# Fused attention and MLP on one core: batch 0 goes through attention by token tiles with all heads

## The chip, the core and the metric

The kernel runs on one core of a Trainium2 chip. The metric is the device time of one execution in microseconds (us). The core has a matmul engine (TensorE, PE in the profile; PEld is its weight loading), two elementwise engines (VectorE, DVE; ScalarE, ACT), a programmable engine (GpSimd, POOL) and a queue engine that mostly issues transfers (SyncE, SP). Each engine runs its own instructions in program order, and semaphores tie them together. On-chip memory is SBUF (128 partitions); TensorE writes into PSUM, whose tiles come from small pools.

## The reference, cut to what matters

The input has 8 batches, 8 heads, 576 tokens and a head size of 64. Attention is causal with a bias from a running sum over tokens; its output, heads side by side, is normalized per token and goes through a two-layer MLP (512 to 2048 to 512) with a residual.

```
scores = scale * np.matmul(q, k.transpose(0, 1, 3, 2))
cum = np.cumsum(np.maximum(s, 0.0), axis=-1)
bias = -(cum[:, :, :, None] - cum[:, :, None, :])
scores = np.where(causal, -1000000000.0, scores + np.minimum(bias, 0.0))
scores = scores - np.max(scores, axis=-1, keepdims=True)
attn = np.exp(scores)
attn = attn / (np.sum(attn, axis=-1, keepdims=True) + 1e-09)
x = np.matmul(attn, v)            # then heads side by side: (8, 576, 512)
mu, var = mean and mean square deviation over the 512 of a token
xn = (x - mu) / np.sqrt(var + 1e-06) * g_ln
out = x + np.maximum(xn @ w_ch1, 0.0) @ w_ch2
```

## The kernel before

The program is written out in order by hand (`manual_schedule`), so each engine's queue is the order of the source. A token sequence of 576 is four tiles of 128 (`NF`) and one of 64 (`TL`).

*Scores.* For each head, `scores` (L304) multiplies keys by queries, transposed: 68 rows, 64 of the head and 4 for the bias. The running sum c is split into three bf16 parts (`c_hi`, `c_mid`, `c_lo`, L634 to L637); three rows beside k hold the parts against ones beside q, and one row of -1 stands against `c_hi`. The buffer `kq` holds these rows for four heads and alternates between two copies. Masked diagonal blocks get a second matmul with `ident` and `maskT` (`pe_mask`, for the first ten heads). ScalarE turns each bank of 512 columns into exponentials in `er` (L323). `pv` (L378) multiplies them with v, extended by a column of ones that gives the row sum; VectorE divides (L397, L399, L406).

*Filling kq.* Heads up to 19 come as pairs: rows are loaded, transposed on TensorE (`tr_kind`, L247) and evacuated by ScalarE and VectorE (`evac_pair`, L262). Bias rows are written by small transfers on SP (`aug`, L207; `constant_rows`, L215). Head 0's bias rows come from matmuls with a selection matrix `pick` (L646 to L660). Later heads have their bias in token rows (`rows`, with `cT` from `bias_tr` and `bias_rows`) and go through a transposing transfer on SP (`tr_rows`, L182), two to six heads ahead.

*The first eight heads.* The loop at L745 takes batch 0 head by head: scores of all 576 queries, a pair's transposes, fillers (`keep_warm`, L565, matmuls whose results nobody reads), then the PV of an earlier head. After the last head the statistics of its columns end, `ln_first` (L464) makes the mean and the normalized rows of all four tiles, and at n = 8 (L771) each tile is transposed (`ln_tr`, L478) and the first quarter of the MLP's first layer follows it, 128 columns at a time (`columns`, L778). The other parts of batch 0's MLP are units of four matmuls of 512 columns in `queue`, two for each head until head 16, and spread evenly over the heads after that (L809). A batch has 32 units: 16 of the first layer (`mlp1`, L493) and 16 quarters of the second (`mlp2`, L511).

*Buffers.* PSUM pools: `ps_s` 3 (scores), `ps_m` 2 (MLP and the first pairs' transposes), `ps_t` 2 (transposes, fillers), `ps_o` 1 (PV, or the bias transposes).

*Transfers.* SP carries float loads and the small bias rows; POOL's queue carries loads that cast to bf16 (`ld_cast`, `ld_cast_v`, `ld_w1`, `ld_w2`), in the order of the source[...].

The softmax here doesn't subtract the row's maximum and nothing guards it: scores larger than these inputs give would overflow.

## Time and profile before

| | us |
|---|---|
| Median of 3 runs | 366.84 |
| The runs | 366.84, 366.32, 371.82 |
| Profiled execution, whole | 368.54 |
| Profiled execution, span from first to last instruction | 366.8 |
| TensorE busy | 355.0 |
| VectorE busy | 202.9 |
| ScalarE busy | 191.3 |
| GpSimd busy | 164.9 |

The span is what the views of the trace divide; the profiled execution's own time is 1.7 us longer. A busy TensorE counts the fillers too, and the ends of matmuls are modelled. In a row of the timeline the first number is the start in the span, the second the length; "L" is the line in the kernel; a bracket names the idle time before an instruction and what ended it. "128*128 128x512" is the stationary operand (rows * columns) and the moving one.

### The profile page before, as it was taken

What the parts mean: (1) busy time and instruction counts of PE and PEld (TensorE: products, weight loads), DVE (VectorE), ACT (ScalarE), POOL (GpSimd) and SP (SyncE); (2) the same over time, 40 slices, a digit from 0 to 9 for tenths busy, and PEclk for the clock granted to TensorE, in tenths of its full rate; (3) what the DMA queues carried; (4) which work ended last, traced back from release to release, by engine and by line L of the source; (5) the groups of instructions that cost most, each with busy time, mean ns of one, the idle gap of its engine ahead of it and who ended that gap; (6) DMA issues with size and microseconds to landing.
All of it is one profiled execution on the core that took longest, in us unless ns stands there. A gap on an engine that the chain in (4) does not pass through costs nothing.

```text
span 366.8 us, 8315 instructions
## 1 busy us (share of the span) xinstructions
PE 355.0 (97%) x3017; PEld 197.1 (54%) x3067; DVE 202.9 (55%) x535; ACT 191.3 (52%) x367; POOL 164.9 (45%) x447
## 2 busy tenths in 40 slices
PE   8998999999999999999999999999999999999995
PEld 3677555565555555555455555555555554444444
DVE  7697789684357554944384547743675483112211
ACT  5895988467732673367534753476337522501410
POOL 8854468667633656344675563554852101000000
PEclk9999999999999999999999999999999999999999
DMA  8999999999965999599979986798830011011013
GB/s 144 162 195 178 202 211 193 163 240 176 183 146 141 206 199 181 104 215 163 188 176 213 194 183 140 189 191 182 174 102 2 0 59 57 1 58 59 0 31 86
DMA packets 156653, 52.17 MB, mean 142 GB/s; under 512 B 143641, under 2 KB 151940, under 8 KB 156612
## 3 DMA queue, kind: packets, MB, share of 16 engines
q1 hardware_dynamic: 138868, 43.08, 55.5%
q0 software_dynamic: 17344, 8.03, 18.9%
q8 instruction: 24, 0.39, 0.5%
q10 hardware_dynamic: 400, 0.52, 0.4%
q14 instruction: 17, 0.14, 0.2%
HBM read 37.11 MB, written 9.44 MB: 127 GB/s over the span
## 4 chain that ended last, share of the span: by engine, by line
PE 72%; DVE 7%; DMA 6%; SPq 4%; POOL 4%; issue 3%; ACT 3%; POOLq 0%; ACTq 0%
PE py L515 26%; PE ph L497 25%; PE pot L389 6%; SPq L164 3%; PE sc L312 3%; PE sa L312 3%; PE sb L312 3%; DMA rowtmp<-in_q_dram 2%; PE idle L568 2%; DMA vtmp<-in_v_dram 2%; DVE xn L451 2%; PE trx L484 2%; DVE stats L423 1%; POOL er L331 1%; ACT er L323 1%
## 5 line engine op out<-in xcount | busy, mean ns | idle before, releaser
L515 PE MATMUL py<-w_bf,hT 128*128 128x512 bf16 (+1 forms) x565 | 132.1, 373 | 1.6 <-DVE yo L524 0.4
L497 PE MATMUL ph<-xT,w_bf 128*128 128x512 bf16 x478 | 116.4, 379 | 1.1 <-DVE yo L524 0.2
L507 ACT ACTIVATE hT<-ph 128x512 bf16<-128x512 f32 x102 | 61.0, 598 | 64.4 <-PE ph L497 64.4
L515 PEld LDWEIGHTS <-hT 128*128 128x128 bf16 x592 | 53.5, 98 | 49.1 <-issue 0.9
L497 PEld LDWEIGHTS <-w_bf 128*128 128x128 bf16 x560 | 50.1, 97 | 51.3 <-issue 2.9
L323 ACT ACTIVATE er<-sa 128x512 bf16<-128x512 f32 x64 | 38.2, 597 | 70.9 <-PE sa L312 50.1
L331 POOL TENSOR_SCALAR_AFFINE_SELECT er<-er 128x128 bf16<-128x128 bf16 x216 | 59.7, 300 | 22.5 <-ACT er L323 22.3
L505 DVE TENSOR_SCALAR hT<-ph 128x512 bf16<-128x512 f32 x38 | 26.3, 692 | 56.7 <-PE ph L497 49.0
L176 POOL CAST rows<-rowtmp 128x512 bf16<-128x512 f32 (+1 forms) x55 | 33.5, 609 | 50.7 <-DMA rowtmp<-in_q_dram 46.0
L312 PEld LDWEIGHTS <-kq 68*128 68x128 bf16 x452 | 33.4, 97 | 27.4 <-issue 1.7
L389 PEld LDWEIGHTS <-er 128*128 128x128 bf16 x960 | 37.5, 98 | 14.9 <-issue 0.7
L389 PE MATMUL pot<-v_bf,er 128*128 128x65 bf16 x960 | 40.2, 193 | 0.5 <-PE sd L355 0.3
L397 DVE RECIPROCAL rinv<-pot 128x5 f32<-128x5 f32 x64 | 12.3, 192 | 49.2 <-PE pot L389 48.9
L323 ACT ACTIVATE er<-sc 128x512 bf16<-128x512 f32 x64 | 39.2, 612 | 0.0
L323 ACT ACTIVATE er<-sb 128x512 bf16<-128x512 f32 x64 | 38.4, 599 | 0.3 <-PE sb L312 0.2
L524 DVE SCALAR_TENSOR_TENSOR yo<-py,rstd,xb 128x512 f32<-128x512 f32 x32 | 23.9, 748 | 26.2 <-PE py L515 19.7
L399 DVE TENSOR_TENSOR xb<-pot,rinv 128x256 f32<-128x256 f32 x64 | 27.2, 425 | 2.2
L102 POOL CAST v_bf<-vtmp 128x512 bf16<-128x512 f32 (+1 forms) x30 | 18.5, 617 | 19.6 <-DMA vtmp<-in_v_dram 19.5
L439 POOL TENSOR_TENSOR rstd<-rstd,mhalf 128x4 f32<-128x4 f32 (+1 forms) x8 | 8.8, 1095 | 38.0 <-DVE rstd L438 37.9
L312 PE MATMUL sc<-kq 68*128 68x256 bf16 (+1 forms) x216 | 25.3, 229 | 0.3
L423 DVE BATCH_NORM_STATS2 stats<-xb 128x6 f32<-128x128 f32 (+2 forms) x100 | 25.3, 313 | 0.4
L312 PE MATMUL sb<-kq 68*128 68x64 bf16 (+1 forms) x172 | 24.5, 244 | 0.9 <-DMA kq<-rows 0.6
(101 smaller groups left out, 322.1 us busy)
## 6 DMA issues: line engine op xcount, KB each, us to landing
out_dram<-yo SPq DMA_DIRECT2D x32, 256.0 KB
vtmp<-in_v_dram SPq DMA_DIRECT2D x24, 256.0 KB
rowtmp<-in_k_dram SPq DMA_DIRECT2D x44, 128.0 KB
rowtmp<-in_q_dram SPq DMA_DIRECT2D x44, 128.0 KB
w_bf<-in_moe_w_ch_dram POOLq DMA_DIRECT2D x8, 512.0 KB, 10.7
kp<-in_k_dram POOLq DMA_DIRECT2D x9, 144.0 KB, 6.8
qp<-in_q_dram POOLq DMA_DIRECT2D x9, 144.0 KB, 7.0
v_bf<-in_v_dram POOLq DMA_DIRECT2D x8, 128.0 KB, 8.1
```

The source lines that it names most:

```text
L176: nc.gpsimd.tensor_copy(out=r[0:pn, :, :, 0:D], in_=loaded.pop(("rows", gam, t))[0:pn])
L312: nc.tensor.matmul(a[:, c + a0 - q0 : c + a1 - q0], lhsT=k_cols(b, h, kb), rhs=cols, start=True, stop=not (pe_mask and diag),)
L323: nc.scalar.activation(out=e[:, o : o + 512], in_=a, func=ACT.Exp, scale=scale)
L331: nc.gpsimd.affine_select(out=e[:, o : o + P], in_=e[:, o : o + P], compare_op=ALU.is_ge, fill=0.0, base=0, pattern=[[1, P]], channel_mult ...
L389: nc.tensor.matmul(pot[:, t, :], lhsT=e[:, o : o + P], rhs=vv[:, kb, h, :], start=(kb == 0), stop=(kb == last),)
L399: nc.vector.tensor_tensor(out=xb[b][:, :, hs], in0=pot[:, 0:NF, 0:D], in1=rinv[:, 0:NF].unsqueeze(2).to_broadcast([P, NF, D]), op=ALU.mult,)
L423: nc.vector.bn_stats(out=st[b][:, t, part, :], in_=x[:, lo:hi])
L497: nc.tensor.matmul(ph, lhsT=w1_bf[:, kd, fb * P : (fb + 1) * P], rhs=xT[:, kd, :], start=(kd == 0), stop=(kd == KD - 1),)
L505: nc.vector.tensor_scalar_max(out=hT[:, fb, :], in0=ph, scalar1=0.0)
L507: nc.scalar.activation(out=hT[:, fb, :], in_=ph, func=ACT.Relu)
L515: nc.tensor.matmul(py[0], lhsT=hT[:, fb, t * P : (t + 1) * P], rhs=w2_bf[:, fb, c0:c1], start=(fb == 0), stop=(fb == FB - 1),)
L524: nc.vector.scalar_tensor_tensor(out=yo, in0=py[0], scalar=rs, in1=x[:, c0:c1], op0=ALU.mult, op1=ALU.add)
```

## The change

Batch 0 no longer goes head by head. Its token rows of k and q are laid beside each other for all heads in `rowb` (128 tokens, 5 tiles, 8 k heads and 8 q heads, 68 columns), with the bias in columns 64 to 67: constants by `memset`, the parts of c by transposes and two copies for each tile (`bias_tr`, `bias_cols`). For this c is summed and split in three column ranges (0 to 128, to 256, to 576). A tile's 16 row blocks of 68 columns are transposed on TensorE (`tr_tile`) and one copy for four heads, 1024 elements a partition, moves them into `kq` (`evac_tile`).

The order is then by query tile t: scores of all eight heads for this tile against keys 0 to t (`tile_bank`, four blocks to a bank), PV for four heads at once (`tile_pv`) with division and statistics, norm of this tile (`ln_xn`, `ln_tr`), and the pieces of the first MLP layer for this tile (`piece`: four column blocks of 128 hidden units). Two of the layer's four quarters are done as pieces, so batch 0 leaves 24 units in `queue` instead of 28, and head 8 runs two units in the common loop. The last 64 tokens have their own functions (`last_bank`, `last_keys`, `last_pv`).

The selection matmuls of head 0, the constant rows, `aug` for the first two groups, `ln_first` and the transfers of pairs 0 to 3 are gone. k and q of tile 0 come as floats on SP with a cast on ScalarE, the other tiles by casting loads on POOL's queue. `aug(2)`, pair 4's transposes and `bias_rows` stand at the end of the new part, pairs 8 and 9 are loaded one head earlier, and the loop starts at head 8. The diff, cut:

```diff
+    rowb = const.tile([P, NT, 2 * H, KA], BF16, name="rowb")
...
+    def tile_src(kind, t):
+        pn = P if t < NF else TL
+        src = k if kind == "k" else q
+        return src[0, :, t * P : t * P + pn, :].rearrange("h s d -> s h d")
+
+    def tile_dst(kind, t):
+        pn = P if t < NF else TL
+        u = "kq".index(kind)
+        return rowb[0:pn, t, u * H : (u + 1) * H, 0:D]
+
+    def ld_tile(kind, t):
+        tmp = stage.tile([P, H, D], F32, name="tiletmp", tag="st")
+        nc.sync.dma_start(out=tmp, in_=tile_src(kind, t))
+        loaded[kind, t] = tmp
+
+    def cast_tile(kind, t, eng):
+        copy_on(eng, tile_dst(kind, t), loaded.pop((kind, t)))
+
+    def ld_cast_tile(kind, t):
+        nc.gpsimd.dma_start(out=tile_dst(kind, t), in_=tile_src(kind, t))
...
+    trc = ps_o.tile([P, 3, NT, BH], BF16, name="trc", tag="pot")
+
+    def bias_tr(t):
+        pn = P if t < NF else TL
         for j, src in enumerate((c_hi, c_mid, c_lo)):
-            for t in range(NT):
-                pn = P if t < NF else TL
-                nc.tensor.transpose(
-                    tr[0:pn, j, t, :], src[:, t * P : t * P + pn], ident[0:BH, 0:BH]
-                )
-        return tr
+            nc.tensor.transpose(
+                trc[0:pn, j, t, :], src[:, t * P : t * P + pn], ident[0:BH, 0:BH]
+            )
+
+
+    def bias_cols(t0, t1, pn=P):
+        nc.vector.tensor_copy(
+            out=rowb[0:pn, t0:t1, 0:H, D + 1 : KA],
+            in_=trc[0:pn, :, t0:t1, 0:H].rearrange("p j t x -> p t x j"),
+        )
+        nc.vector.tensor_copy(out=rowb[0:pn, t0:t1, H : 2 * H, D], in_=trc[0:pn, 0, t0:t1, 0:H])
+
+
+    def cum_scan(c0, c1):
+        nc.vector.tensor_tensor_scan(
+            out=c_sc[:, c0:c1],
+            data0=c_one[:, c0:c1],
+            data1=c_in[:, c0:c1],
+            initial=0.0 if c0 == 0 else c_sc[:, c0 - 1 : c0],
+            op0=ALU.mult,
+            op1=ALU.add,
+        )
+
+    def cum_relu(c0, c1):
+        nc.vector.tensor_scalar(
+            out=c_in[:, c0:c1],
+            in0=c_in[:, c0:c1],
+            scalar1=0.0,
+            scalar2=1.0 / scale,
+            op0=ALU.max,
+            op1=ALU.mult,
+        )
+
+    def cum_split(c0, c1):
+        x, y, hi, mid, lo = (a[:, c0:c1] for a in (c_sc, c_in, c_hi, c_mid, c_lo))
+        nc.vector.tensor_copy(out=hi, in_=x)
+        nc.vector.tensor_tensor(out=y, in0=x, in1=hi, op=ALU.subtract)
+        nc.vector.tensor_copy(out=mid, in_=y)
+        nc.vector.tensor_tensor(out=lo, in0=y, in1=mid, op=ALU.subtract)
...
-        if g < 5:
-            tr = ps_m.tile([P, S], BF16, name="trqk", tag="m")
-        else:
-            tr = ps_t.tile([P, S], BF16, name="trqk", tag="tr")
+        tr = ps_t.tile([P, S], BF16, name="trqk", tag="tr")
...
+        pool, tag = (ps_m, "m") if b == 0 else (ps_t, "tr")
+        tr = pool.tile([P, KD, P], BF16, name="trx", tag=tag)
...
-    ld_pair("k", 0)
-    ld_pair("q", 0)
-
-    ONE2 = 1.0019378662109375
-    NEG2 = -1.0058441162109375
+    ld_tile("k", 0)
+    ld_tile("q", 0)
...
-    keep_warm(12)
+    keep_warm(9)
...
+    for t in range(1, NF):
+        ld_cast_tile("k", t)
+        ld_cast_tile("q", t)
+        ld_cast_v(0, t - 1)
+    ld_cast_v(0, NF - 1)
+    ld_w1(0)
+    ld_cast_tile("k", NF)
+    ld_cast_tile("q", NF)
+    ld_cast_v(0, NF)
+    ld_w1(1)
+    ld_cast_pair(4)
+    nc.gpsimd.memset(v_bf[1][:, 0:NF, :, D : D + 1], 1.0)
+    nc.gpsimd.memset(v_bf[1][0:TL, NF, :, D : D + 1], 1.0)
+    for i in range(2):
         nc.gpsimd.memset(v_bf[i][TL:P, NF, :, :], 0.0)
     nc.gpsimd.memset(er[TL:P, :, OD : OD + TL], 0.0)
     nc.gpsimd.memset(er[:, :, OD + TL : EW], 0.0)
+    ld_cast_pair(5)
+    ld_w1(2)
     for t in range(NT):
+        ld_cast_v(1, t)
+    ld_w1(3)
...
+    def tr_tile(t):
+        pn = P if t < NF else TL
+        for g in range(2):
+            tr = ps_m.tile([P, 2, G, P], BF16, name="trt", tag="m")
+            for u in range(2):
+                for hh in range(G):
+                    nc.tensor.transpose(
+                        tr[0:KA, u, hh, 0:pn],
+                        rowb[0:pn, t, u * H + g * G + hh, :],
+                        ident[0:pn, 0:pn],
+                    )
+            trt[t, g] = tr
...
+    def evac_tile(t, g, eng):
+        pn = P if t < NF else TL
+        copy_on(
+            eng,
+            kq[g][0:KA, :, :, t * P : t * P + pn],
+            trt.pop((t, g))[0:KA, :, :, 0:pn],
+        )
+    def tile_bank(t, g, i):
+        a = ps_s.tile([P, 512], F32, name="st", tag="s")
+        for c in range(4):
+            hh, kb = divmod(4 * i + c, t + 1)
+            nc.tensor.matmul(
+                a[:, c * P : (c + 1) * P],
+                lhsT=kq[g][0:KA, 0, hh, kb * P : (kb + 1) * P],
+                rhs=kq[g][0:KA, 1, hh, t * P : (t + 1) * P],
+                start=True,
+                stop=kb < t,
+            )
+            if kb == t:
+                nc.tensor.matmul(
+                    a[:, c * P : (c + 1) * P], lhsT=ident, rhs=maskT, start=False, stop=True
+                )
+        o = (0, 2, 6, 0)[t] + g * (t + 1) + i
+        nc.scalar.activation(out=er_slot(o), in_=a, func=ACT.Exp, scale=scale)
...
+    def tile_pv(t, g):
+        pot = ps_t.tile([P, G, D + 1], F32, name="pot0", tag="tr")
+        for hh in range(G):
+            for kb in range(t + 1):
+                i, c = divmod(hh * (t + 1) + kb, 4)
+                o = (0, 2, 6, 0)[t] + g * (t + 1) + i
+                nc.tensor.matmul(
+                    pot[:, hh, :],
+                    lhsT=er_slot(o)[:, c * P : (c + 1) * P],
+                    rhs=v_bf[0][:, kb, g * G + hh, :],
+                    start=(kb == 0),
+                    stop=(kb == t),
+                )
+        rinv = small.tile([P, NT], F32, name="rinv", tag="rinv")
+        nc.vector.reciprocal(out=rinv[:, 0:G], in_=pot[:, :, D])
+        x = xb[0][:, t, g * 256 : (g + 1) * 256]
+        nc.vector.tensor_tensor(
+            out=x.rearrange("p (h d) -> p h d", d=D),
+            in0=pot[:, :, 0:D],
+            in1=rinv[:, 0:G].unsqueeze(2).to_broadcast([P, G, D]),
+            op=ALU.mult,
+        )
+        nc.vector.bn_stats(out=st[0][:, t, g, :], in_=x)
...
+    def last_bank(g, i):
+        a = ps_s.tile([P, 512], F32, name="st", tag="s")
+        for hh in range(G):
+            for w in range(2):
+                kb, c = 2 * i + w, (2 * hh + w) * TL
+                nc.tensor.matmul(
+                    a[:, c : c + TL],
+                    lhsT=kq[g][0:KA, 0, hh, kb * P : (kb + 1) * P],
+                    rhs=kq[g][0:KA, 1, hh, NF * P : S],
+                    start=True,
+                    stop=True,
+                )
+        nc.scalar.activation(out=er_slot(8 + 2 * g + i), in_=a, func=ACT.Exp, scale=scale)
...
+    def last_pv(g):
+        pot = ps_t.tile([P, G, D + 1], F32, name="pot0", tag="tr")
+        for hh in range(G):
+            for kb in range(NT):
+                h = g * G + hh
+                if kb < NF:
+                    c = (2 * hh + kb % 2) * TL
+                    e = er_slot(8 + 2 * g + kb // 2)[:, c : c + TL]
+                    vv = v_bf[0][:, kb, h, :]
+                else:
+                    e = er_slot(0)[0:TL, h * TL : (h + 1) * TL]
+                    vv = v_bf[0][0:TL, kb, h, :]
+                nc.tensor.matmul(
+                    pot[0:TL, hh, :], lhsT=e, rhs=vv, start=(kb == 0), stop=(kb == NF)
+                )
+        rinv = small.tile([P, NT], F32, name="rinv", tag="rinv")
+        nc.vector.reciprocal(out=rinv[0:TL, 0:G], in_=pot[0:TL, :, D])
+        nc.vector.tensor_tensor(
+            out=xm[0][0:TL, g * 256 : (g + 1) * 256].rearrange("p (h d) -> p h d", d=D),
+            in0=pot[0:TL, :, 0:D],
+            in1=rinv[0:TL, 0:G].unsqueeze(2).to_broadcast([TL, G, D]),
+            op=ALU.mult,
+        )
...
+    def piece(c, t, eng):
+        ph = ps_m.tile([P, 4, P], F32, name="ph", tag="m")
+        cols = slice(t * P, (t + 1) * P)
+        for j in range(4):
+            fb = 4 * c + j
+            for kd in range(KD):
+                nc.tensor.matmul(
+                    ph[:, j, :],
+                    lhsT=w1_bf[:, kd, fb * P : (fb + 1) * P],
+                    rhs=xTs[0][:, kd, cols],
+                    start=(kd == 0),
+                    stop=(kd == KD - 1),
+                )
+        dst = hT[:, 4 * c : 4 * c + 4, cols]
+        if eng == "act":
+            nc.scalar.activation(out=dst, in_=ph, func=ACT.Relu)
+        else:
+            nc.vector.tensor_scalar_max(out=dst, in0=ph, scalar1=0.0)
...
+    R = (P, 2 * P, S)
+    cum_relu(0, R[0])
+    cum_scan(0, R[0])
+    cum_split(0, R[0])
+    cast_tile("k", 0, "act")
+    cast_tile("q", 0, "act")
+    cum_relu(R[0], S)
+    bias_tr(0)
+    bias_cols(0, 1)
+    cum_scan(R[0], R[1])
+    cum_split(R[0], R[1])
+    keep_warm(1)
+    tr_tile(0)
+    evac_tile(0, 0, "act")
+    bias_tr(1)
+    evac_tile(0, 1, "dve")
+    bias_cols(1, 2)
+    cum_scan(R[1], S)
     keep_warm(2)
+    banks(0, 0, 0)
+    banks(0, 1, 0)
+    tr_tile(1)
+    evac_tile(1, 0, "act")
+    evac_tile(1, 1, "dve")
+    cum_split(R[1], S)
+    tile_pv(0, 0)
+    tile_pv(0, 1)
+    banks(1, 0, 0, 1)
+    for t in (2, 3, 4):
+        bias_tr(t)
+    bias_cols(2, NF)
+    bias_cols(NF, NT, TL)
+    banks(1, 1, 0, 1)
+    tr_tile(2)
+    evac_tile(2, 0, "act")
+    evac_tile(2, 1, "dve")
+    keep_warm(2)
+    banks(2, 0, 0, 1, 2)
+    tile_pv(1, 0)
+    tile_pv(1, 1)
+    ln_xn(0, 0)
+    tr_tile(3)
+    evac_tile(3, 0, "dve")
+    evac_tile(3, 1, "dve")
+    banks(2, 1, 0, 1, 2)
+    ln_xn(0, 1)
+    keep_warm(2)
+    banks(3, 0, 0, 1)
+    tile_pv(2, 0)
+    ln_tr(0, 0, "act")
+    banks(3, 0, 2, 3)
+    tile_pv(2, 1)
+    ln_xn(0, 2)
+    piece(0, 0, "dve")
+    banks(3, 1, 0)
+    ln_tr(0, 1, "act")
+    banks(3, 1, 1)
+    piece(0, 1, "dve")
+    banks(3, 1, 2, 3)
+    tile_pv(3, 0)
+    ln_tr(0, 2, "act")
+    piece(0, 2, "dve")
+    tile_pv(3, 1)
+    ln_xn(0, 3)
+    tr_tile(4)
+    evac_tile(4, 0, "act")
+    evac_tile(4, 1, "dve")
+    piece(1, 0, "act")
+    last_bank(0, 0)
+    last_bank(0, 1)
+    piece(1, 1, "dve")
+    last_bank(1, 0)
+    ln_tr(0, 3, "act")
+    last_bank(1, 1)
+    piece(1, 2, "dve")
+    last_keys()
+    aug(2, nc.sync)
+    piece(0, 3, "act")
+    tr_pair(4)
+    evac_pair("k", 4, ("dve", "dve"))
+    evac_pair("q", 4, ("act", "act"))
+    piece(1, 3, "dve")
+    last_pv(0)
+    last_pv(1)
+    bias_rows(trc)
+    queue = batch_units(0)[8:]
```

## The prediction

> **What bounds the kernel now.** I read the page first, then the chain of waits up to 80 us, then busy time by windows cut at stages, then the timelines of TensorE and VectorE to 72 us.
>
> ```profile
> span 366.8 us, 8315 instructions
> ...
> PE 355.0 (97%) x3017; PEld 197.1 (54%) x3067; DVE 202.9 (55%) x535; ACT 191.3 (52%) x367; POOL 164.9 (45%) x447
> ```
>
> TensorE sets the end, but part of its 97% is filler (`keep_warm`, tile `idle`). Windows (columns: stretch, length, busy PE, PEld, DVE, ACT, POOL, clock, DMA share, GB/s) show that only the start can give anything:
>
> ```profile
> 11.04:28.44 17.40, 16.33 (x262) 12.24 (x264) 13.76 (x39) 16.34 (x34) 12.37 (x20) 1.00 1.79 179
> 28.44:31.65 3.21, 2.83 (x23) 1.52 (x24) 3.04 (x16) 2.24 (x3) 1.45 (x3) 1.00 2.15 154
> 63.46:80.58 17.12, 16.93 (x160) 9.75 (x160) 13.37 (x41) 8.86 (x20) 9.55 (x26) 1.00 0.93 192
> ```
>
> From 63 us TensorE is full with real work (16.93 of 17.12). From 11 to 28.4 ScalarE is full (16.34 of 17.40: the exponentials and half the evacuations). Then the chain leaves TensorE (start, length):
>
> ```profile
> 1.26 5.30 PE idle L568 x12
> ...
> 20.50 0.45 PE pot L389 x15
> ...
> 28.38 0.52 DVE stats L423 x4
> ...
> 30.84 1.43 DVE xn L451 x2
> 32.31 0.40 PE trx L484 x4
> ...
> 34.00 0.89 PE ph L782 x16
> ```
>
> The norm of batch 0 waits for its last head; TensorE meanwhile runs 15 transposes and fillers. The state to compare is the top of head 9:
>
> ```profile
> 29.76 1.67 PE L568 MATMUL idle<-zeros 128*128 128x512 bf16 x7 [0.16 <-issue]
> ...
> 39.24 0.42 PE L255 MATMUL trqk<-ident,kp 96*128 96x96 bf16 x6
> ```
>
> At 39.24 batch 0's attention and head 8's scores are done, and 27 of batch 0's 32 MLP units remain. The change reaches the same place with 22 (24 queued, two run in head 8). A unit is four 512-column matmuls, 8 in 1.73 us, so 0.864. Break-even is 39.24 + 5 x 0.864 = 43.56 us.
>
> [...] The change transposes rows 68 wide and uses 64-wide stationaries for the last tile; the trace has just three such loads, in the bias transposes (groups by form, 28 to 30 us: count, busy, mean ns):
>
> ```profile
> L227 PE MATMUL trc<-ident,c 64*128 64x64 bf16 x12 | 0.9, 192 | 0.3 <-DVE xm L406 0.3
> L227 PE MATMUL trc<-ident,c 64*64 64x64 bf16 x3 | 0.6, 213 | 0.0
> ```
>
> [...] these 15 run from 28.44 to 29.53, 1.09 us, where 15 matmuls of 65 columns with wide weights take 0.45 (the chain above, L389). So (1.09 - 0.44)/3, about 0.21 us more, for each narrow load standing among wide ones. [...] here the first 12 fillers take 5.30 us, half speed. [...] the trace's bf16 copy of 512 from PSUM took 0.42 us against 0.69 for a float one, so 1024 elements cost 0.70.
>
> **The change part by part.**
> *Start.* Bias, head 0's selection matmuls, constant rows and early `aug` DMAs go; scan and split come in column ranges. c lands at 3.94 as now; 128 columns need relu 0.22, scan 0.40, split 1.05 (scaled from 0.60, 1.35, 2.5 for 576), bias transposes at 5.7. k and q of tile 0 come as 256-byte pieces, 1024 each:
>
> ```profile
> q1 hardware_dynamic: 2849, 0.71, 108.4%
> ...
> q0 software_dynamic: 4129, 0.57, 213.8%
> ```
>
> The first line is 58 to 61 us: 950 such packets per us. With issue at 1.5 and 2.1 as now and the landing delay of the old pairs (k used at 5.61), q lands near 6.6; cast 0.6; first transposes 7.3, against 6.97 now. The second line is 9 to 13 us: about 1030 packets per us from POOL's queue, so a k, q or v tile costs 1.0 us. Ten of them from POOL, issued from 1.9 on at 0.9 each, land from 7.6 (k1) to 16.1 (v3); tile t's transposes want theirs at 10.4, 16.7, 19.9, so the transfers are covered by 2 to 6 us. w1 parts land by 19 and 23, first used at 25.7. `gb` comes earlier; nothing waits for it.
>
> *TensorE's work from 7.3 to the top of head 9*, at 0.056 us per 128 columns (L782, 16 in 0.89) and 0.031 per 64/65:
> 80 row transposes x 0.060 + 5 runs x 0.2 = 5.8; 80 score blocks and 32 masks x 0.056 = 6.2; last tile's scores 1.0, keys 1.1; 80 PV x 0.031 = 2.5; last PV 40 x 0.060 + 0.2 = 2.6; norm transposes 0.9; eight pieces x 16 x 0.056 = 7.1; bias 0.4; fillers 1.3; pair 4 0.5; head 8 with two units 2.75. Sum 32.2. [...]
>
> What this replaces up to 39.24: 25 fillers after the first 12 (0.216 each, 5.4), head 0's selection matmuls and gaps of some 3 us go, which is all there is to win; the pairs' transposes (eight sets at 0.26, 2.1) become 5.8, scores 5.8 become 8.3, PV 3.6 becomes 5.1.
>
> *Waits.* VectorE gets a long serial queue. What it will do for every tile it does now once for every head (timeline of VectorE: start, length):
>
> ```profile
> 23.12 0.20 DVE L397 RECIPROCAL rinv<-pot 128x5 f32<-128x5 f32 x1 [0.34 <-PE pot L389]
> 23.35 0.42 DVE L399 TENSOR_TENSOR xb<-pot,rinv 128x256 f32<-128x256 f32 x1
> ...
> 23.88 1.39 DVE L423 BATCH_NORM_STATS2 stats<-xb 128x6 f32<-128x256 f32 x4
> ...
> 35.15 0.42 DVE L100 COPY xT<-trx 128x512 bf16<-128x512 bf16 x1 [1.57 <-PE trx L484]
> 36.49 1.29 DVE L799 TENSOR_SCALAR hT<-ph 128x512 bf16<-128x512 f32 x2 [0.92 <-PE ph L782]
> ```
>
> Each product waits for its reciprocal and each statistic for its product, so a PV drain is 0.22 + 0.44 + 0.36 = 1.0, eight of them; a norm 0.18 + 0.74, four; five evacuations 0.70 (last 0.4); five piece drains 0.64; splits 1.75 for 320 columns. Followed in program order:
> tile 0/1 evacuations and ScalarE's (1024 elements, 0.98) 0.7; the 320-column split stands behind tile 1's evacuation at 12.4 and ends at 14.2, the bias transposes of tiles 2-4 wait 1.3; then two drains and the bias copies until 16.6, tile 2's row transposes wait 1.5; its evacuation 0.3; tile 3's evacuation stands behind two drains and a norm and ends at 23.6, its scores wait 1.2; pieces wait for a PSUM buffer of two behind norm and drains 0.8 + 0.8; tail 0.3, 0.2 and 0.7 (last PV, behind pair 4's evacuation). Sum 7.8. ScalarE has 20 us idle in this stretch; exponentials no longer bound it.
>
> *Sum.* 7.3 + 32.2 + 7.8 = 47.3, 3.8 past break-even. Only 9 fillers run before a gap: [...] I take 0.4. Total +4.2.
>
> *Edits at nothing.* `aug(2)` now waits for the last keys' scores (39.1): four SP issues of 0.6 and about 2 us of landing end at 43.5, head 8 needs them at 44.7; less cover costs what is late. Nothing useful stands behind them on SP. `bias_rows` (2.0 on VectorE) moves from head 9 to before head 8, beside scores and a unit. POOL's later loads keep order; `rstd`'s power holds POOL until 34, w2 is first used about 55. Heads 16-19 have 8 units instead of 13: row transposes for head 20, last issued at 71.56 and used at 80.58, lose 4.3 of 9.0 us cover.
>
> The profiled execution took 368.54 (span 366.8): it becomes 372.7. The median of the runs shown, 366.84, becomes 371.0.
>
> **Rivals.**
> *Narrow loads serialize (slower).* If each waits until the previous matmul has left, as both sides of the three did, a step is 0.144 (64 columns) or 0.17 (128). Row transposes 64 x 0.17 + 16 x 0.144 = 13.2 (+7.4), keys 2.3 (+1.2), last PV 5.8 (+3.2): +11.8, of which 1.4 fills waits: 381.4. It passes 2% (7.3 us; about what a measurement of this kernel can tell) from 0.09 per step. For: no narrow load in the trace overlaps. Against: both sides of each were switches, which a run has once. If instead a run costs nothing but its switch, 369.
> *Transfers late.* If POOL's tile loads take 1.6 times as long, sharing engines with k, q and `gb`, tiles 2 and 3 start late by 2.8: 373.8. Against: nothing else is queued after 7 us.
> *Faster.* If VectorE keeps up and the 7.8 of waits vanish, 39.5 against 43.56: 362.8; it decides where waits stay under 4.0. For: VectorE's work is less than TensorE's. Against: two PSUM buffers and the program's order.
>
> **How the numbers follow.** Forecast 371.0, chance 0.53, own range 368 to 374; serial 0.31; late transfers 0.08; faster 0.06; else 0.02. Range 366 to 382 leaves out the fast case and the serial tail. Slower by over 2% (374.2): 0.31, part of the transfers, the forecast's tail: 0.38; faster by over 2%: 0.03; the rest 0.59.
>
> **What would show it.** Row transposes starting at 7.3; 16 of them in 1.2 us (2.7 if serial); tile 2's start near 16.7 waiting on VectorE's bias copy, not on DMA; last PV 1.3 us a half; head 9 at 47. I am wrong if head 9 comes before 44 or after 52, or if heads 16-19 show idle TensorE.

## The result and the profile after

The changed kernel takes 378.59 us (median of 4 runs, 377.44 to 380.07) against 366.73 for the kernel before beside it (4 runs): a ratio of 1.033, 95% interval 1.0284 to 1.0375. The ratio leaves out one slow run of the kernel before, of 371.82. The change makes it 11.9 us slower; the forecast was +4.2 (371.0, range 366 to 382). Its profiled execution took 378.56. The page of the changed kernel: span and the granted clock in 40 slices of 9.4 us (a 9 is full speed, or nearly so):

```profile
span 376.9 us, 8560 instructions
...
PEclk9899969999999999999999999999999999999999
```

The clock has dips in the second and the sixth slice. The windows of the changed kernel (columns as in the prediction) put them in two short stretches:

```profile
16.03:24.01 7.98, 6.76 (x84) 5.72 (x85) 4.36 (x14) 4.16 (x7) 6.05 (x12) 0.79 1.50 188
...
42.84:53.07 10.23, 8.43 (x62) 4.85 (x62) 4.19 (x10) 1.95 (x4) 0.85 (x2) 0.69 1.19 183
```

The stretch of the last line holds the last PV, a hole and head 8. The top of head 9 comes at 53.07, where the forecast had 47.3 and the break-even point was 43.56. The chain of waits of the changed kernel (start, length) says what the hole is:

```profile
40.84 1.15 SPq L223
...
42.03 5.62 DMA kq<-c
...
47.78 0.58 PE sa L347
```

The path leaves every compute engine. It runs from the last keys' scores (39.26) to SP's four issues of `aug(2)` (from 39.38) and then lies 5.62 us in the last of the four transfers (four rows of 1152 bytes each), while the last PV is done 1.8 us before head 8 can start. TensorE's timeline for the same stretch, and one run of row transposes:

```profile
10.43 1.05 PE L658 MATMUL trt<-ident,rowb 128*68 128x128 bf16 x16
11.32 0.42 PE L704 MATMUL pot<-v_bf,er 128*128 128x65 bf16 x8
...
42.84 3.14 PE L765 MATMUL pot<-v_bf,er 128*64 128x65 bf16 x40 [0.85 <-ACT kq L96]
47.78 0.58 PE L347 MATMUL sa<-kq 68*128 68x512 bf16 x1 [1.80 <-DMA kq<-c]
...
49.44 1.91 PE L516 MATMUL ph<-xT,w_bf 128*128 128x512 bf16 x4
```

Two readings. Sixteen narrow row transposes go from 10.43 to the next matmul at 11.32, so 0.055 us each: they overlap (the pieces' 128 columns with 128 wide weights step by 0.056). And the first MLP unit of head 8 takes 1.91 us (the second 1.89), where the runs below show 1.02: half speed, from head 8's start to 53.6.

So the forecast's state is missed by 5.8 us, and the trace splits it: the last PV ended at 46.0 instead of 44.7 (+1.3), head 8 waited 1.8 us for the transfer, and from its scores to the top of head 9 it took 5.3 instead of 2.6 us (+2.7). Two theories were put on trial. *Transfer and clock*: the late bias rows cause both the wait and, through the idle stretch, the half clock. *Thin work*: narrow and short matmuls cost TensorE the time and pull the clock down themselves.

### The profile page after: what moved, and what is told of

It reads as the page before. It is cut to its first block, busy times and chain, and to the rows that moved or that the text cites. A ratio compares the mean times of both kernels' runs of the same rounds, so it can differ in the third digit from the quotient of the medians.

```text
span 376.9 us, 8560 instructions
## 1 busy us (share of the span) xinstructions
PE 359.9 (96%) x3189; PEld 204.8 (54%) x3189; DVE 202.7 (54%) x532; ACT 187.0 (50%) x357; POOL 167.4 (44%) x447
## 4 chain that ended last, share of the span: by engine, by line
PE 82%; DVE 10%; DMA 3%; ACT 2%; issue 1%; SPq 1%; ACTq 0%; DVEq 0%
PE ph L516 31%; PE py L534 29%; PE pot L423 6%; DVE xn L484 3%; PE sc L347 3%; PE sa L347 3%; PE sb L347 3%; PE trx L503 2%; DMA kq<-c 1%; PE ph L784 1%; DMA tiletmp<-in_q_dram 1%; DVE stats L457 1%; PE trt L658 1%; DVE yo L543 1%; DVE kq L98 1%
## 5 line engine op out<-in xcount | busy, mean ns | idle before, releaser
L534 PE MATMUL py<-w_bf,hT 128*128 128x512 bf16 (+1 forms) x592 | 136.5, 373 | 0.5 <-DVE yo L543 0.5
L358 ACT ACTIVATE er<-sa 128x512 bf16<-128x512 f32 x56 | 33.4, 596 | 72.3 <-PE sa L347 43.1
L347 PEld LDWEIGHTS <-kq 68*128 68x128 bf16 x412 | 29.9, 98 | 24.3 <-issue 3.6
L423 PEld LDWEIGHTS <-er 128*128 128x128 bf16 x840 | 33.0, 98 | 13.3 <-issue 0.3
L423 PE MATMUL pot<-v_bf,er 128*128 128x65 bf16 x840 | 34.7, 193 | 0.0
L358 ACT ACTIVATE er<-sc 128x512 bf16<-128x512 f32 x56 | 34.3, 613 | 0.0
L358 ACT ACTIVATE er<-sb 128x512 bf16<-128x512 f32 x56 | 33.6, 600 | 0.0
L100 POOL CAST v_bf<-vtmp 128x512 bf16<-128x512 f32 (+1 forms) x30 | 18.8, 627 | 15.6 <-DMA vtmp<-in_v_dram 14.3
L484 DVE SCALAR_TENSOR_TENSOR xn<-xb,mv,gb 128x512 bf16<-128x512 f32 x32 | 24.3, 761 | 1.1
L433 DVE TENSOR_TENSOR xb<-pot,rinv 128x256 f32<-128x256 f32 x56 | 23.8, 424 | 1.9
L347 PE MATMUL sa<-kq 68*128 68x512 bf16 x56 | 21.6, 385 | 1.8 <-DMA kq<-c 1.8
```

The lines of the kernel that those rows point to most:

```text
L347: nc.tensor.matmul(a[:, c + a0 - q0 : c + a1 - q0], lhsT=k_cols(b, h, kb), rhs=cols, start=True, stop=not (pe_mask and diag),)
L358: nc.scalar.activation(out=e[:, o : o + 512], in_=a, func=ACT.Exp, scale=scale)
L423: nc.tensor.matmul(pot[:, t, :], lhsT=e[:, o : o + P], rhs=vv[:, kb, h, :], start=(kb == 0), stop=(kb == last),)
L433: nc.vector.tensor_tensor(out=xb[b][:, :, hs], in0=pot[:, 0:NF, 0:D], in1=rinv[:, 0:NF].unsqueeze(2).to_broadcast([P, NF, D]), op=ALU.mult,)
L484: nc.vector.scalar_tensor_tensor(out=xn, in0=tiles[t], scalar=mvs[b][:, t, 0:1], in1=gb, op0=ALU.subtract, op1=ALU.mult,)
L534: nc.tensor.matmul(py[0], lhsT=hT[:, fb, t * P : (t + 1) * P], rhs=w2_bf[:, fb, c0:c1], start=(fb == 0), stop=(fb == FB - 1),)
```

## The experiments

**Fillers in the hole.** The transfer stays late; TensorE is kept busy.

```diff
     last_pv(1)
+    keep_warm(7)
     bias_rows(trc)
```

> The changed kernel with seven 512-column filler matmuls (1.5 us at full clock) between the last PV and head 8; the transfer stays late. Theory (the half clock from 47.8 to 53.5 is left by the idle stretch before it): head 8's scores still near 47.8, at full speed, head 9 near 50.4, 375.9 (-2.7). Rival (the clock falls already during the last PV, whose small matmuls keep the array thin): the fillers take 0.43 each, end near 49, and head 9 comes at 52 to 54, 377.5 to 379.5. Neither touches the rest.

377.17 us, ratio 1.027 (1.0246 to 1.0294). In its timeline:

```profile
46.01 1.69 PE L586 MATMUL idle<-zeros 128*128 128x512 bf16 x6
47.82 0.38 PE L347 MATMUL sa<-kq 68*128 68x512 bf16 x1
...
50.57 0.42 PE L290 MATMUL trqk<-ident,kp 96*128 96x96 bf16 x6
```

The fillers (six of the seven are in the trace) run at full speed right behind the last PV, so the thin matmuls had not taken the clock down by then. Head 8 starts where it did and runs at full speed; head 9 comes 2.5 us earlier, as expected. The profiled execution (375.99) gains all of it; the median only 1.4: two of the four executions show a mean clock of 0.986 and 0.991 instead of 0.995.

**The last PV with 128 rows.** In the changed kernel's groups by form, eight of the 40 matmuls of the last PV contract over 64 rows:

```profile
L765 PE MATMUL pot<-v_bf,er 64*64 64x65 bf16 x8 | 1.7, 214 | 0.0
```

In the order of their starts the 128-row ones step by 0.03 to 0.05 us, but the one with 64 rows starts 0.126 behind its predecessor and the next one 0.145 behind it. The edit multiplies the other 64 rows by the zeros that v already holds there:

```diff
-                    e = er_slot(0)[0:TL, h * TL : (h + 1) * TL]
-                    vv = v_bf[0][0:TL, kb, h, :]
+                    e = er_slot(0)[:, h * TL : (h + 1) * TL]
+                    vv = v_bf[0][:, kb, h, :]
```

> The changed kernel with the fifth matmul of each head in the last PV contracting over 128 rows instead of 64 (the added v rows are zero). In the changed kernel the last PV's 40 matmuls took 3.1 us: the four of a head with 128 rows step by 0.03 to 0.05, but the one with 64 rows starts 0.126 after its predecessor and the next one 0.145 after it. Theory (a change in the number of rows costs the overlap, and head 8 waits for the bias transfer anyway): last PV 1.3 to 1.5 us, but head 8's scores stay at 47.8 and the time at 378.6 within 0.7. Rival (the narrow 64-column loads are what costs): last PV still about 3 us. Rival (TensorE's work counts, not the transfer): 376.9.

378.77 us, ratio 1.0309 (1.0289 to 1.0328): no change, and yet the timeline has

```profile
42.79 1.43 PE L765 MATMUL pot<-v_bf,er 128*64 128x65 bf16 x40 [0.85 <-ACT kq L96]
47.96 0.58 PE L347 MATMUL sa<-kq 68*128 68x512 bf16 x1 [3.75 <-DMA kq<-c]
```

The last PV shrinks from 3.1 to 1.4 us with the same 64-column weights, so what cost it was the switch between 64 and 128 rows, not narrow loads. (68 and 128 rows alternate in the last keys at 0.032 us a step, so not every change of rows costs this.) All of the gain becomes wait: 1.80 turns into 3.75. TensorE's work was not what bound this place.

**A third kq buffer.** Heads 8 to 11 get a buffer of their own, so `aug(2)` need not wait for the last keys (`KQ` gives each group of four heads its buffer). For room, `cT` takes the place of the used `rowb`; two memsets on GpSimd fill the constant rows, and SP issues `aug(2)` from 31.85 on.

```diff
-    kq = [const.tile([P, 2, G, SP], BF16, name=f"kq{i}") for i in range(2)]
+    kq = [const.tile([P, 2, G, SP], BF16, name=f"kq{i}") for i in range(3)]
+    KQ = (0, 1, 2, 1) + (0, 1) * 6
...
     cum_split(R[1], S)
+    aug(2, nc.sync)
...
     last_keys()
-    aug(2, nc.sync)
```

> The changed kernel with a third kq buffer for heads 8 to 11 (its constant rows set by two small memsets on POOL behind the last w1 load, near 28 us; cT takes the place of the used rowb, so that it fits), so that aug(2) no longer waits for the last keys' scores and is issued near 28 us instead of 39.4. In the changed kernel head 8's scores waited 1.8 us for that transfer (landed 47.6, last PV ended 45.9), and TensorE then ran at half speed until 53.5. Theory (late bias transfer, and the half clock is what the gap before head 8 leaves behind): head 8's scores start right behind the last PV near 46, at full clock, head 9 at 48.6 instead of 53.1, time 374.1 (-4.5). Rival (the clock falls anyway, from the thin work before): scores near 46 at half speed, head 9 near 51.2, 376.7. Rival (the transfer hid another wait, such as pair 4's copies or a score buffer): head 8 still near 47.8 and 378.6.

374.11 us, ratio 1.0188 (1.0157 to 1.0219), the number of the theory. Its timeline:

```profile
42.56 3.14 PE L768 MATMUL pot<-v_bf,er 128*64 128x65 bf16 x40 [0.80 <-ACT kq L97]
45.64 0.39 PE L348 MATMUL sa<-kq 68*128 68x512 bf16 x1
...
48.39 0.42 PE L291 MATMUL trqk<-ident,kp 96*128 96x96 bf16 x6
```

Head 8 follows the last PV without a bracket and at full speed. The same thin work stands ahead of it, so thin work alone does not explain the half clock; its share in it is estimated further below.

**Both.** The third buffer and the 128-row last PV, the two diffs above together.

> The third kq buffer, and the last PV's 64-row matmuls made 128 rows high (which alone shortened the last PV from 3.1 to 1.4 us and left the time at 378.8). Theory (once the transfer is off the path, TensorE's own work is what is left): last PV ends near 44.3, head 9 near 46.9, 372.4 (-6.2). Rival (another wait is next, VectorE's copies of pair 4 or the drain of the last PV): no better than the third buffer alone, 374.

372.54 us, ratio 1.014 (1.0109 to 1.0171). Its timeline:

```profile
43.26 1.43 PE L768 MATMUL pot<-v_bf,er 128*64 128x65 bf16 x40 [0.80 <-ACT kq L97]
...
47.38 0.42 PE L291 MATMUL trqk<-ident,kp 96*128 96x96 bf16 x6
```

The edit that gave nothing alone gives 1.6 in the median here (the runs of the two kernels overlap), since the last PV is now on the path: from its start to head 9 it takes 4.1 us, where the third buffer alone took 5.8.

**Why the transfer was slow.** The last four packets took over 5 us. The DMA view of the changed kernel from 38 to 46 us:

```profile
q0 software_dynamic: 1292, 1.08, 101.4%
...
w_bf<-in_moe_w_ch_dram POOLq DMA_DIRECT2D x4, 512.0 KB, 11.8
```

POOL had been held by `rstd` until 36.8 and then issued loads for pairs 6 to 8 and four parts of w2, some 3 MB in 7 us, before and during the issues of `aug(2)`. The edit holds those loads back until the three k rows of `aug(2)` have landed:

```diff
         if n == 8:
+            nc.gpsimd.tensor_copy(out=warm[D : D + 4, 0:1], in_=kq[0][D : D + 4, 0, 0, 0:1])
             ld_cast_pair(6)
```

> The changed kernel, with a tiny POOL copy that reads a row written by aug(2) placed ahead of POOL's loads of pairs 6 and 7 and of w2: these 3 MB, issued from 36.8 to 43.7 in the changed kernel, now wait until aug(2) has landed. aug(2) itself is issued as before, at 39.4 to 42.6. Theory (its 16 packets of 1152 bytes take 5 us to land because all 16 DMA engines are full with POOL's loads): it lands within 2.5 us of its last issue, near 45, so that head 8 starts at the last PV's end near 46; full clock or nearly so, head 9 near 48.6 to 50, 374 to 376. Rival (so many small packets from SP take 5 us by themselves): landing still at 47.6, time 378.6. Cost: POOL's loads come up to 8 us later; pair 6 is wanted near 60 and w2 near 70, so nothing waits.

375.99 us, ratio 1.0228 (1.0195 to 1.026); its profiled execution (374.84) is the lowest of the four. The DMA view of this kernel from 38 to 46 us (queue, packets, MB, share of the engines' time):

```profile
q0 software_dynamic: 8, 0.01, 1.5%
```

its chain, and POOL's copy that waits for the rows:

```profile
43.53 3.14 PE pot L765 x40
46.67 0.32 PE sa L347
```

```profile
43.98 0.18 POOL L896 CAST warm<-kq 4x1 f32<-4x1 bf16 x1 [6.47 <-DMA kq<-c]
```

With POOL's queue empty the packets of each transfer come some 1.4 us after its issue starts (the fourth issued at 42.13, its packets at 43.4 to 43.5). POOL's copy, which waits for it, runs 1.85 us after the start of the issue; in the changed kernel the transfer took 5.62. Head 8 follows the last PV. The issues end at 42.7, in the changed kernel at 42.6; only the neighbours are gone. On SP's queue the same transfer took 1.85 us without POOL's loads and 5.6 beside them, so its landing is no constant; how the engines share their time between the two queues was not shown.

This number could have been read before the prediction. In the kernel before, SP issued the four transfers of `aug(3)` from 26.57 to 29.4 us. Its DMA view from 29 to 31.6 us lists no packet on SP's queue, q1:

```profile
q0 software_dynamic: 792, 0.41, 199.1%
```

and the one from 31.6 to 33.6 has

```profile
q1 hardware_dynamic: 64, 0.03, 7.6%
```

The packets of 1152 bytes came from 31.8 to 33.5: the first 5.2 us after the first issue began (26.57), the last 5.1 after the last one did (28.4), with loads of pairs and weights in the queue there too. Nothing waited for them: head 12, which needs them, starts at 49.05.

**Fillers ahead of tile 2's row transposes**, on top of both edits.

```diff
     banks(1, 1, 0, 1)
+    keep_warm(5)
     tr_tile(2)
```

> Third kq buffer, 128-row last PV, and five 512-column fillers (1.1 us at full clock) in the 0.9 us gap ahead of tile 2's row transposes, after which the changed kernel ran at half speed from 16.0 to 19.3. Theory (the clock falls for the gap, but this stretch is bound by VectorE, whose evacuations TensorE waits for 1.2 us at 24): tile 2's 16 row transposes take 0.9 instead of 1.9 us, but head 9 comes only 0 to 0.5 us earlier than without the fillers. Rival (TensorE's lost 1.6 us count in full): head 9 and the time 1.6 us earlier. Rival (the clock has already fallen there): the fillers take 0.43 each and cost about 1 us.

371.89 us, ratio 1.0127 (1.0085 to 1.0169), not told apart from 372.54. From the bias transposes of tile 2 to head 9 it took 33.5 us with the fillers and 33.0 without, and tile 3's scores still waited:

```profile
26.75 0.40 PE L682 MATMUL st<-kq 68*128 68x128 bf16 x4 [1.43 <-DVE kq L99]
```

Here the fillers came too late: the clock was at half from 16.9 to 20.3, from before the first of them, as the second rival had it. So this run doesn't show the stretch at full speed. It shows that tile 2's scores, 0.9 us later from the bias transposes on, put head 9 back by only 0.5: VectorE's evacuation ends this stretch.

**The order of VectorE's and ScalarE's queues.** With the transfer gone, 5 us are left of the loss. The forecast put its waits down to the order of VectorE's queue. This kernel keeps the work, moves one evacuation of tile 3 (0.7 us) from VectorE to ScalarE, and changes the order (`tile_pv` now ends with the matmuls, and `drain` is its VectorE part):

```diff
     bias_cols(2, NF)
     bias_cols(NF, NT, TL)
+    drain(0, 0)
+    drain(0, 1)
...
-    ln_xn(0, 0)
     tr_tile(3)
-    evac_tile(3, 0, "dve")
+    evac_tile(3, 0, "act")
     evac_tile(3, 1, "dve")
+    drain(1, 1)
```

> Third kq buffer and 128-row last PV as before (372.5), and the order of VectorE's and ScalarE's work in batch 0 changed, with no instruction added or dropped but two fillers: the bias copies of tiles 2 to 4 stand ahead of tile 0's drains, the norms of tiles 0 and 1 in VectorE's free stretches, tile 3's two evacuations on ScalarE and VectorE ahead of the second drain of tile 1, pieces 0 of tiles 1 and 2 one score bank or one PV later, pair 4's transposes and copies ahead of the last banks of heads 4 to 7. Theory (what is left of the loss against the kernel before is the waits that the forecast counted, 7.8, and they come from the order in the queues, not from the amount of work): of the waits seen with the third buffer (0.85 and 0.22 at tile 2, 1.6 of half clock behind them, 1.43 at tile 3, 0.71 and 0.72 at the pieces, 0.80 at the last PV) 3 to 5 us go; head 9 near 42 to 44, time 367.5 to 369.5, level with the kernel before. Rival (VectorE's amount of work bounds the stretch, so that a wait only moves): under 1.5 us gained, 371 to 372.5.

372.66 us, ratio 1.0131 (1.0074 to 1.0188): nothing gained in the median, but two executions took 371 at a mean clock of 0.995 and two 374.4 at 0.986. The profiled one is of the latter. Its trace shows tile 3's scores at 21.63 instead of 23.79 (third buffer alone), and then a wait of TensorE of 2.33 us, up to 41.36, for ScalarE's copy into `xT`. A placing of this experiment cost these 2.3 us of the lead: half of pair 4's q copy on ScalarE stood 3.6 us behind VectorE's copies into the same buffer, and the last norm's copy stood behind it. The clock cost more of it: it was at half from 32.3 to 35.7 and from 42.5 to 46.0, with TensorE busy throughout, up to 1.7 us each time.

**The order, mended.** ScalarE copies q alone, and tile 3's norm stands behind tile 4's evacuation.

```diff
-    evac_pair("q", 4, ("dve", "act"))
+    evac_pair("q", 4, ("act", "act"))
```

> The changed order again, with two placings of it mended: pair 4's q is copied by ScalarE alone (its second half had waited 3.6 us for VectorE's copies, with the exponentials of heads 4 to 7 and the last norm's copy behind it: TensorE idle for 2.3 us at 41), and the norm of tile 3 stands behind tile 4's evacuation on VectorE. The changed order had been 2.2 us ahead of the third-buffer kernels at tile 3's scores (21.6 against 23.8) and lost it from 31 on. Theory (the waits come from the order): the lead is kept and grows, head 9 near 42 to 44, time 368 to 370. Rival (the amount of VectorE's work): head 9 at 46 or later, 371 to 372.5.

368.94 us, ratio 1.0048 (1.0031 to 1.0065), with

```profile
43.23 0.42 PE L291 MATMUL trqk<-ident,kp 96*128 96x96 bf16 x6
```

That is 3.6 us less than both edits without the order. From tile 2's bias transposes (13.66; with both edits alone 14.37) to head 9 it takes 29.6 us instead of 33.0, with no instruction removed but two fillers. The evacuation that went to ScalarE accounts for at most 0.7 of this; the rest of the gain is order, not the amount of VectorE's work.

**A filler more at two places of the start.**

```diff
-    keep_warm(1)
+    keep_warm(2)
     tr_tile(0)
...
-    keep_warm(2)
+    keep_warm(3)
     banks(0, 0, 0)
```

> The same with one filler more ahead of tile 0's row transposes (at 6.1) and one more ahead of tile 0's scores. In the changed-order kernel's profiled execution the clock was at half until 12.4 (two of its four timed runs show 0.986 and 374.4, two 0.995 and 370.9), since nine fillers and a gap don't always open it. Theory (the first window of the clock decides): the spread between runs shrinks, all runs near the lower value, median 0.5 to 2 us lower than without. Rival (which window opens the clock depends on its phase at the start, not on one filler): same spread, same median within 0.7.

369.15 us, ratio 1.0048 (1.0033 to 1.0063). The median stays, as the rival had it; the four runs lie closer (368.5 to 369.3, against 368.1 to 370.0), too few to say more.

**More placings**, and fillers at the c split.

```diff
+    keep_warm(3, ps_s, "s")
     for t in (2, 3, 4):
         bias_tr(t)
...
-    banks(3, 1, 1, 2)
+    banks(3, 1, 1, 2, 3)
     piece(0, 1, "dve")
-    banks(3, 1, 3)
...
-    tr_tile(4)
+    tr_tile(4, (0,))
     evac_tile(4, 0, "act")
+    tr_pair(4)
+    tr_tile(4, (1,))
```

> The second changed order (368.9; head 9 at 43.2) with three more placings: pair 4's transposes between the two halves of tile 4's row transposes, where TensorE waited 0.67 for a PSUM buffer, and its copies ahead of the last banks, so that the last norm's copy is no longer behind them (0.59); piece 0 of tile 1 behind the last bank of tile 3 (0.43); and three fillers where TensorE waits for the c split at 12.7 to 13.7, since the clock fell to half from 14.9 to 17.9 without an idle stretch over 0.4 us. Theory (each of these waits is TensorE's own now, since VectorE has slack after the reordering): up to 1.7 from the placings and 1 to 1.7 from the clock, head 9 at 40.5 to 42, time 366 to 367.5, level with the kernel before or just under it. Rival (the waits move on, and the fall of the clock there is not a matter of these fillers): 368 to 369.

368.82 us, ratio 1.0039 (1.0015 to 1.0062): not told apart. Tile 4's wait of 0.67 is gone, but the last pieces now wait 0.68 for VectorE's `hT`, and head 9 is at 42.73. The waits moved on.

**The kernel before once more**, to see where its profiled execution had lost 1.7 us against its median.

> The kernel before, unchanged, profiled once more. The execution that the forecast was summed against took 368.54 (span 366.8), 1.7 above its median, while the changed kernel's profiled execution (378.56) is its median. Theory: the forecast's difference of +4.2 was taken from a reference state that was itself 1 to 2 us late, so that here the span is near 365.2 and the top of head 9 comes near 37.6 instead of 39.24, the rest from there on being the same 327.6. Rival: the 1.7 us lie behind head 9; then head 9 is at 39.2 again.

367.58 us in this execution, span 365.9, and head 9 as before:

```profile
39.01 0.42 PE L255 MATMUL trqk<-ident,kp 96*128 96x96 bf16 x6
```

The rival is right. The reference state was sound; against this execution the first one lost 0.2 us by head 9 and 1.0 more between heads 24 and 48.

This second profile also shows what head 9 left out. Windows from the start of head 16 to that of head 22, of the kernel before (second profile) and of the changed kernel:

```profile
63.23:89.55 26.32, 26.29 (x243) 14.77 (x240) 17.63 (x52) 15.96 (x33) 16.75 (x46) 1.00 0.96 193
```

```profile
77.52:101.03 23.51, 22.48 (x222) 12.80 (x219) 16.51 (x50) 15.97 (x33) 17.71 (x46) 1.00 0.95 200
```

TensorE idles 1.0 us where it idled none. The five units that the change had done early should give back 4.32 us; the lag between the two kernels falls from 14.3 at head 9's scores to 11.5 at head 24's, so 2.8 come back. In the trace the norm transposes of batch 1 wait for VectorE's `xn` at two places; counted from start to start these cost 1.5 us, which is what is missing.

**Two units kept for heads 16 to 19**, on top of the third order.

```diff
-        run_units(1)
+        run_units(0 if n in (10, 12) else 1)
```

> The third changed order (368.8) with one MLP unit of batch 0 fewer in each of heads 10 and 12, so that heads 16 to 19 find 10 units in the queue instead of 8 (13 in the kernel before). Where the changed kernels have five units fewer left at the top of head 9, 4.32 us should come back by head 24; only 2.4 to 2.8 do, and their traces show TensorE idle for 0.80 and 0.55 us in heads 18 and 19, at the norm transposes of batch 1, waiting for VectorE's xn. Theory (with five units fewer these transposes come before their norm is done; the work moved there fills the wait): heads 10 and 12 each 0.86 shorter, the idle of heads 18 and 19 under 0.4 in sum, time 0.8 to 1.3 lower, 367.5 to 368.0, level with the kernel before. Rival (heads 9 to 15 are bound by ScalarE, whose copies of the pairs fill 20.8 of 24.3 us there, so that TensorE would wait for it instead): no change, 368.5 to 369.

369.05 us, ratio 1.0049 (1.0034 to 1.0065): no gain. Of the two waits the one of 0.80 is gone and the one of 0.55 stays, and heads 10 and 12 got 0.64 and 0.65 shorter instead of 0.86. By head 20 this kernel had gained 0.3 us on the one without the edit; it had lost 0.4 again by head 24 and lost 1.0 more in head 24, where the second bank of scores (101.80) shows a wait of 0.84 for its transposing transfer, `kq<-rows`. Whether the edit made that transfer late stays open. No version beat the kernel before.

## Why the prediction was right or wrong

*Right: the row transposes.* Taken at 0.060 us, which no trace of the kernel before showed, measured 0.055 in a run. The rival with the second largest chance, serial narrow loads, asked for 0.17 and is out: a run of narrow loads overlaps. That the measured 378.6 lies nearer to its 381.4 than to 371.0 is chance. The three narrow loads of the kernel before, its only evidence, were switches of width, as the prediction's own argument against it said; the changed kernel's last keys, 64 weight columns wide, show 0.149 and 0.126 us at the two ends of the run and 0.032 a step inside.

*Right, in part by luck: the timetable up to the last keys.* Transposes at 6.91 (7.3), tile 2's start at 16.03 behind VectorE's bias copy (16.7), tile 3's scores waiting 1.22 (1.2), the pieces 0.71 and 0.72 (0.8 and 0.8), the last PV 0.85 (0.7); a full evacuation took VectorE 0.68 (0.70) and ScalarE 1.01 (0.98), in the median; TensorE's waits up to the last PV add to 6.5 (7.8). That these come from the order of VectorE's queue was only argued; the second reordering showed it for most of 3.4 us. But the work between these points took 32.6 us where the sum has 29.5: half speed from 16.0 to 19.4 is 1.7 of the difference, the last PV 0.5, and 0.9 stay unassigned. Shorter waits and an earlier start hid about half of it.

*Mis-sized: the last PV.* 3.1 us instead of 2.6, and for another reason than the narrow loads it was priced by (0.060 a step, again shown by no trace of the kernel before): eight times 0.2 us for a matmul over 64 rows between those over 128, and 1.4 in all without them.

*Failed: "four SP issues of 0.6 and about 2 us of landing".* This stood under the edits at nothing. The issues took 0.57 to 0.77, but for one of 1.15. The landing, put at about 2 us behind the last issue, took 5.0 from its end (5.6 from its start), beside 3 MB of POOL's loads. The forecast named the cover (1.2 us) and that "less cover costs what is late", but did not look at which transfers would be in flight then. A transfer put from 18 us, where it had slack, to the end of the path needed its landing time in the company it would have. The third buffer and the quiet queue each showed it: head 8 behind the last PV at once.

*Failed: the clock.* The forecast charged 0.4 for the start, its author's estimate with no trace behind it, and nothing later. Behind the wait of 1.8 us head 8 ran at half speed: 5.3 us, where the filler run has 2.75, so 2.5 lost, more than the wait itself. The clock fell 0.8 us after the end of the thin last PV (45.98, 46.75). Windows of the changed kernel, cut where the clock changes:

```profile
43.34:46.75 3.41, 2.64 (x35) 1.98 (x33) 1.29 (x5) 0.00 (x0) 0.35 (x1) 1.00 1.13 158
46.75:53.58 6.83, 5.80 (x28) 2.96 (x29) 2.46 (x5) 2.22 (x5) 0.00 (x0) 0.50 1.22 198
```

The length of a gap does not sort the cases. In the kernel with the mended order the clock fell at 14.62 (0.50 up to 18.04) with no gap over 0.4 us in the 3.41 us ahead; in the changed kernel a gap of 1.22 before tile 3's scores left it at full speed (1.00 from 19.45 to 46.75). In all 14 traces, half speed that came after the first opening of the clock and before the end of the program comes in stretches of 3.41 us or twice that (the two of the kernel before have none), and the changes within one execution lie on a grid of 3.41 us. An estimate from the traces' records, of which a few are missing: in the 3.41 us ahead of a fall TensorE streamed 2015 to 3712 columns of moving operands, in those that kept the full clock 3264 or more, where a full one reaches some 8000. The two ranges overlap, so no threshold is shown. The stretch ahead of the fall at 46.75 held 2015, the thin last PV and the wait together; in the third buffer's kernel and the filler kernel, with head 8 or fillers right behind the PV, the same stretch held 3998 columns or more by that estimate, and the clock stayed.

*Failed, smaller: heads 16 to 19.* The forecast asked whether the row transposes for head 20 kept their cover. They did; the norm transposes of batch 1, which the five units had covered too, did not. About 1.5 us of the 4.3 credited did not come back. Idle TensorE there and head 9 after 52 were the forecast's own signs of being wrong; both came.

*The sum.* Against the state at head 9: 1.3 before the last PV's end, 1.8 of wait, 2.7 in head 8, nearly all of it half speed, together 5.8 (53.07 less 47.3). At head 9 the kernel is 13.8 us behind, 9.5 after the credit of 4.3. Heads 16 to 19 add 1.5, and the 1.0 that the first profiled execution of the kernel before lost later takes some back: +10.0 from profiled execution to profiled execution, where 4.2 was forecast. The other 1.8 of the 11.9 in medians is the first profiled execution of the kernel before, 1.7 above its own median; the changed kernel's was at its median. The forecast carried its difference over as if both stood alike. With the transfer repaired and the last PV at full rows the kernel is at +5.0, near the forecast's 4.2. That is in part luck: the last PV is then 1.2 under its term, and heads 16 to 19 are 1.5 over theirs.

## What to carry to other kernels

A small transfer that moves from a place with slack to the end of a path must be priced by the landing of the same transfer among the same neighbours, read from the packets in the trace, and not by its size; another buffer that let it start early was worth 4.5 us here, a speed-up of the work ahead of it alone nothing. A short wait of TensorE between thin matmuls can cost twice, once as idle time and again as half clock afterwards (1.8 and 2.5 us here), so fillers in a wait that can't be removed can pay (2.5 us in one execution here, 1.4 in the median). Work that is done early takes cover away from whatever was hidden behind it later; follow the credit to the place where it was to be spent.

## What the runs showed of the hardware

- A run of matmuls with 64 or 68 weight columns overlaps like one with 128 (0.032 us a step for the last keys with 64, 0.055 for the row transposes with 68; with 128 it is 0.032 for the 65 columns of a PV and 0.056 for the 128 of a piece); a single matmul over 64 rows between ones over 128 starts 0.126 us behind its predecessor and holds its successor for 0.145, where 0.03 is the step without the switch. Matmuls over 68 and over 128 rows alternate at 0.032 without this cost.
- A transfer of four rows of 1152 bytes from SP shows its packets 1.4 us after the start of its issue with POOL's queue empty, and 5.1 to 5.2 us after it in the kernel before, with POOL's loads on the 16 DMA engines (their packets took 199.1% of the engines' time from 29 to 31.6 us). What waited for it went on after 1.85 us with the queue empty and after 5.6 in the changed kernel.
- TensorE fell to half speed and came back on a grid of 3.41 us (16.03 to 19.45 and 46.75 to 53.58 in the changed kernel). It fell where the 3.41 us before held 2015 to 3712 streamed columns (estimated from the records); the longest gap in them or across their end was 0.4 us in one execution and 3.75 in another. Whether a run shows it differs from execution to execution of one kernel: mean clock 0.982 to 0.986 in the changed kernel's, 0.986 to 0.995 in those of the filler run.
